# Keys and queries turned by VectorE in 32x32 pieces, pooling on VectorE, fewer GpSimd sums, maxima turned before they are loaded, a new table of places

## The chip, the cores and the metric

One core of a Trainium2 chip runs the kernel. The metric is the device time of one execution in microseconds (us); the numbers below come from three timed runs and from one more execution that was profiled.

## What is computed

Attention with queries pooled in pairs, then a mixing layer. The attention is the part that the change touches (8 batches, 8 heads, 1152 positions, 64 columns a head):

```python
q_pool = q.reshape(B, H, S // 2, 2, D).mean(axis=3)          # 576 pooled queries
scores = np.matmul(q_pool, k.transpose(0, 1, 3, 2)) / np.sqrt(D)
scores = scores - np.max(scores, axis=-1, keepdims=True)
attn = np.exp(scores)
attn = attn / (np.sum(attn, axis=-1, keepdims=True) + 1e-09)
x = np.matmul(attn, v)                                       # then laid out as 8 x 576 x 512
theta = x @ w_theta                                          # the mixing layer, untouched here
y = w_tok_r @ (x * np.cos(theta)) + w_tok_i @ (x * np.sin(theta))
u = x + y
out = u + np.maximum(u @ w_ch, 0.0)
```

## The kernel before

Two heads of one batch are a pair; there are 32 pairs, 0 to 31. A first stage does the attention of all pairs, a second the mixing layer of the 8 batches; the change lies in the first. One pair goes through these steps:

- **Loads** (SyncE, `q` L228, `k` L238, `v` L252). Pooling adds neighbouring queries: `pool_q` (L246), on VectorE for pair 0 and on GpSimd for the others.
- **Turning.** Scores need the 64 columns of a head on the partitions, so TensorE turns keys and pooled queries into PSUM (`prep_t`, tile `pt`, L277): 6 key blocks in a first group (g = 0); 6 query blocks and 3 key blocks in a second (g = 1). That is 15 matrix instructions a pair. ScalarE rounds them to `hi` (L293) and VectorE keeps the rest, `lo` (L304); two small copies make `tail` (L300).
- **Maxima** (`maxpass`, tile `pm`, L317, with VectorE's `mx`, L324, 12 blocks a pair, and `px`, `py` for the last queries). `max_nm` (L345) reduces them to 9 columns `nm` on 128 partitions, and `load_max` (L351, L352) brings these with four small DMAs into one row a head, `nmr`.
- **Scores** (`escore`, tile `pe`, L371): for each half `u` of the queries and each of 9 key tiles four products, one of which subtracts the maximum from `nmr`; ScalarE's exponential `pc` (L374). In the text a group of these 8 matmuls is a score group; there are 18 a pair.
- **Sums** (`ssum`, L383): GpSimd adds the first `TAIL` tiles of `pc` into `ss`; TensorE adds the others and sums over the keys (`norm_sum`, tile `pns`, L419).
- **Values** (`av`, tile `pa`, L397): 18 matmuls, 36 instructions, for each half. After that come the division (`xu`, L468), VectorE's 32x32 turn of the result (`xb`, L473) and the stores (L491, L494).

The order on each engine is written out by hand: each step has a place (`MAX_AT`, `PREP_AT`, `AV_AT`, `PLAN` and so on), counted in score groups from the pair's first one, 18 to a pair, and the steps are issued in the order of their places. An engine works strictly in that order. PSUM has four slots of two banks for all of it; `bank2` gives a new tile the slot that a small reckoning (`HOLD`) calls free first, so a late reader of a slot holds up whoever gets the slot next. The loads have one buffer each for `q` and `k`, two for `v`. Beside the pairs the weights of the second stage are prepared step by step (`weights`: in all 18 chunks with four VectorE operations each, L536 to L546).

Of the kernel before, what the change touches and what calls it, by code (L numbers as in the profile page):

```python
# [30 lines left out]
W_END = 30
TURN_AT = 10.275
PRO = ((-34.75, -25.8, -18.2), (-6.0, -5.0, 3.15), (3.75,))
MAX_AT0 = (-25.75, -25.25, -24.75, -24.25, -24.15, -23.25, -22.0, -21.95, -21.75, -21.25, -20.75, -20.25)
MAX_AT1 = (-22.567, -21.371, -20.761, -15.823, -13.312, -12.915, -10.876, -9.537, -8.039, -7.894, -7.714, -7.649)
PLAN = {'load_q': -54.727, 'load_k': -43.238, 'pool_q': -43.609, 'load_max': -3.244, 'load_v': -11.696, 'max_nm': -7.412, 'norm_spread': 32.09, 'norm_load': 34.755, 'norm_recip': 36.124, 'norm_save': 36.922, 'norm_bcast': 37.251, "norm_out": 46.61, "norm_turn": 46.640, 'norm_store': 56.838}
# [3 lines left out]
HOLD = {'e': (8.18, 'a', 3.247), 'pm': (4.108, 'd', 7.636), 'pt': (4.417, 'ad', 1.781), 'px': (5.029, 'd', 5.465), 'py': (6.765, 'd', 0.595), 'pa': (5.964, 'a', 0.05), 'mt': (7.562, 'a', 5.572), 'ns': (4.451, 'a', 3.778), 'pw': (2.473, 'ad', 6.596)}  # L40
# [44 lines left out]
def pooled_attention_moe_kernel(  # L85
# [114 lines left out]
    with ExitStack() as p1:  # L200
# [10 lines left out]
        nmrs = [nrm.tile([P, 5 * P], F32R, name=f"nmr_{n}") for n in range(2)]  # L211
# [12 lines left out]
        def load_q(i):  # L224
            b, hp = divmod(i, NP)
            h0 = 2 * hp
            qn = inp.tile([QP, 2, QT, 2, D], F32, tag="qn", name=f"qn{i}")
            nc.sync.dma_start(  # L228
                qn, q[b, h0 : h0 + 2].rearrange("h (p t f) d -> p h t f d", t=QT, f=2)
            )  # L230
            state[i] = dict(qn=qn)

        def load_k(i):
            b, hp = divmod(i, NP)
            h0 = 2 * hp
            kn = inp.tile([P, KT, 2, D], F32, tag="kn", name=f"kn{i}")
            for h in range(2):
                nc.sync.dma_start(kn[:, :, h, :], k[b, h0 + h].rearrange("(p t) d -> p t d", t=KT))  # L238
            state[i]["kn"] = kn

        def pool_q(i):
            qn = state[i]["qn"]
            qp = state[i]["qp"] = inp.tile([QP, QT, 2, D], F32, tag="qp", name=f"qp{i}")
            eng = nc.vector if i == 0 else nc.gpsimd
            for h in range(2):
                eng.tensor_tensor(qp[:, :, h, :], qn[:, h, :, 0, :], qn[:, h, :, 1, :], ALU.add)  # L246
# [807 lines left out]
```

## Time and profile before

| | us |
|---|---|
| median of three runs (1321.48 to 1322.57) | 1321.58 |
| the profiled execution | 1321.95 |
| its span from the first to the last instruction | 1320.2 |
| TensorE busy in the span | 1288.2 |
| VectorE busy | 847.7 |
| ScalarE busy | 665.7 |
| GpSimd busy | 895.4 |

How to read the rows further down: PE is TensorE, PEld its weight loads, DVE VectorE, ACT ScalarE, POOL GpSimd, SP SyncE. A row of windows gives, for a stretch of the span, each engine's busy time with the number of its instructions in brackets, TensorE's granted clock as a share of full speed, the mean busy share of the 16 DMA engines, and GB/s. A row of the timeline begins with the start and the duration; several instructions of one line are merged, so the distance to the next row's start tells what they cost their engine when it does not wait.

### The profile page before, as it was taken

Reading aid. Unit: us, or ns where it says so; the run is one execution under the profiler, and the core shown is the slowest. Engines: PE = TensorE matmul, PEld = TensorE weight load, DVE = VectorE, ACT = ScalarE, POOL = GpSimd, SP = SyncE. Lnnn points to the kernel's source line nnn. Section 1 sums busy time; section 2 is a strip of 40 time slices with the busy share of each in tenths; the row PEclk is TensorE's granted clock in tenths of the full one; section 3 lists DMA queues with packets and bytes.
Section 4 is the critical chain, followed back from the end, with each engine's and each line's share of the span. In section 5 each row is a group of like instructions: output and inputs, shape, how many; then the busy total and the mean of one; then the engine's idle time right before and its main releaser. Section 6 shows DMA issues by size and latency. Waiting matters only on the chain.

```text
span 1320.2 us, 29458 instructions
## 1 busy us (share of the span) xinstructions
PE 1288.2 (98%) x11850; PEld 1083.3 (82%) x11850; DVE 847.7 (64%) x1151; ACT 665.7 (50%) x1162; POOL 895.4 (68%) x664
## 2 busy tenths in 40 slices
PE   5999999999999999999999999999999999999998
PEld 3877787778787778787777777678899999999997
DVE  6766777676767686776777686545555636647452
ACT  1555555556565656565656555454443433434430
POOL 1799899999898998889998988834333333232310
PEclk7999999999999999999999999999999999999999
DMA  5335444444444444434544423225515335154231
GB/s 131 102 95 139 106 122 116 117 127 117 119 116 130 112 119 118 122 104 117 134 116 119 119 69 96 70 82 131 101 29 100 53 74 111 26 97 78 52 46 37
DMA packets 283209, 131.05 MB, mean 99 GB/s; under 512 B 247024, under 2 KB 247152, under 8 KB 283072
## 3 DMA queue, kind: packets, MB, share of 16 engines
q1 hardware_dynamic: 282896, 128.71, 40.0%
q8 instruction: 93, 1.52, 0.5%
q0 software_dynamic: 176, 0.46, 0.1%
q14 instruction: 44, 0.36, 0.1%
HBM read 97.21 MB, written 30.70 MB: 97 GB/s over the span
## 4 chain that ended last, share of the span: by engine, by line
PE 89%; DVE 4%; ACT 3%; DMA 1%; issue 1%; POOL 1%; SPq 0%; POOLq 0%; ACTq 0%; DVEq 0%
PE pe L371 21%; PE pa L397 21%; PE py L874 15%; PE pm L317 8%; PE pr L913 7%; PE pth L786 7%; PE pt L277 4%; PE pns L419 3%; DVE mx L324 2%; PE px L334 1%; ACT pc L374 1%; ACT Z L843 1%; DMA kn<-in_k_dram 0%; DMA xn<-xbd 0%; PE pwt L600 0%
## 5 line engine op out<-in xcount | busy, mean ns | idle before, releaser
L383 POOL TENSOR_TENSOR ss<-ss,pc 128x576 f32<-128x576 f32 x376 | 548.5, 1459 | 33.0 <-ACT pc L374 7.7
L324 DVE TENSOR_REDUCE mx<-pm 128x2 f32<-128x768 f32 x384 | 358.4, 956 | 204.6 <-PE pm L317 204.5
L374 ACT ACTIVATE pc<-pe 128x576 f32<-128x576 f32 x576 | 344.7, 652 | 79.1 <-PE pe L371 64.2
L397 PE MATMUL pa<-pc,vn 128*64 128x288 f32 x2304 | 294.1, 409 | 0.0
L397 PEld LDWEIGHTS pa<-pc,vn 128*64 128x64 f32 x2304 | 160.1, 137 | 119.1 <-DVE nm L345 7.4
L874 PE MATMUL py<-wtk,Z 128*128 128x288 f32 x1728 | 233.4, 295 | 0.0
L874 PEld LDWEIGHTS py<-wtk,Z 128*128 128x128 f32 x1728 | 231.9, 189 | 1.3
L847 POOL TENSOR_TENSOR Z<-ab,Z 128x512 fp32r<-128x512 f32 x40 | 52.1, 1303 | 257.3 <-ACT Z L843 242.0
L317 PE MATMUL pm<-hi 64*128 64x384 f32 x768 | 174.0, 464 | 4.7 <-ACT hi L293 2.1
L371 PE MATMUL pe<-hi 64*128 64x288 f32 x1152 | 174.1, 296 | 2.9 <-ACT pc L374 1.7
L371 PE MATMUL pe<-nmr,oner 64*128 64x288 f32 x1152 | 172.2, 292 | 1.6 <-DMA nmr<-nm 1.6
L371 PE MATMUL pe<-lo,hi 64*128 64x288 f32 x1152 | 172.2, 293 | 0.0
L371 PE MATMUL pe<-hi,lo 64*128 64x288 f32 x1152 | 172.1, 293 | 0.0
L317 PEld LDWEIGHTS pm<-hi 64*128 64x128 f32 x768 | 118.2, 306 | 35.3 <-issue 26.0
L409 ACT COPY xu<-pa 128x288 f32<-128x288 f32 x64 | 25.5, 399 | 212.9 <-PE pa L397 212.9
L371 PEld LDWEIGHTS pe<-hi 64*128 64x128 f32 x1152 | 113.6, 192 | 7.2 <-ACT pc L374 2.6
L383 POOL TENSOR_TENSOR ss<-pc,pc 128x576 f32<-128x576 f32 x64 | 92.3, 1442 | 31.9 <-ACT pc L374 31.6
L371 PEld LDWEIGHTS pe<-nmr,oner 64*128 64x128 f32 x1152 | 110.6, 185 | 2.0 <-DMA nmr<-nm 1.9
L371 PEld LDWEIGHTS pe<-hi,lo 64*128 64x128 f32 x1152 | 110.2, 185 | 0.0
L371 PEld LDWEIGHTS pe<-lo,hi 64*128 64x128 f32 x1152 | 110.0, 185 | 0.0
L913 PEld LDWEIGHTS pr<-us,wch 128*128 128x128 f32 x768 | 104.2, 189 | 1.7
L913 PE MATMUL pr<-us,wch 128*128 128x288 f32 x768 | 105.1, 295 | 0.0
(99 smaller groups left out, 1499.5 us busy)
## 6 DMA issues: line engine op xcount, KB each, us to landing
qn<-in_q_dram SPq DMA_DIRECT2D x32, 576.0 KB
kn<-in_k_dram SPq DMA_DIRECT2D x64, 288.0 KB
vn<-in_v_dram SPq DMA_DIRECT2D x32, 576.0 KB
dn<-ro SPq DMA_DIRECT2D x64, 144.0 KB
xd<-xu SPq DMA_DIRECT2D x32, 288.0 KB
xbd<-xb SPq DMA_DIRECT2D x32, 288.0 KB
xT<-xd SPq DMA_DIRECT2D x8, 1152.0 KB
xn<-xbd SPq DMA_DIRECT2D x140, 64.0 KB
```

Of the source, the lines that this page charges most:

```text
L277: nc.tensor.transpose(out=pt[:, n, c : c + R], in_=src.rearrange("p h d -> p (h d)"), identity=ident[0:R, 0:R],)
L317: nc.tensor.matmul(pm[:, h, 0:W], hi[hs, Q0 : Q0 + 4 * P].rearrange("d (p j) -> d j p", j=4)[:, j], hi[hs, K0[3 * g] : K0[3 * g] + W], sta ...
L324: nc.vector.tensor_reduce(mx[:, j : j + 5 : 4, g : g + 1], pm[:, :, 0:W], AX.X, ALU.max)
L371: nc.tensor.matmul(pe[:, h, 0:HALF], w[hs], x[hs], start=(n == 0), stop=(n == 3))
L374: nc.scalar.activation(pcs[u, kt], pe[:, :, 0:HALF], AF.Exp, scale=SC)
L383: nc.gpsimd.tensor_tensor(st["ss", u], first, st["pc"][u, kt], ALU.add)
L397: nc.tensor.matmul(pa[hs, 0, 0:HALF], st["vn"][:, h, kt, :], st["pc"][u, kt][:, h, :], start=(kt == 0), stop=(kt == KT - 1),)
L419: nc.tensor.matmul(px[a : a + 32, 1, 0:HALF], ones, sets[u][n][:, h, :], start=(n == 0), stop=(n == len(sets[0]) - 1), tile_position=(0, a),)
L786: nc.tensor.matmul(th, xs[c][:, j * P : (j + 1) * P], ws[:, c], start=(n == 0), stop=(n == 11))
L847: engine("zlo", b).tensor_tensor(Z[1], t, Z[0].bitcast(F32), ALU.subtract)
L874: nc.tensor.matmul(st["py", c, u][:, 0:HALF], Z[zi][:, c * P : (c + 1) * P], wtk[wi][:, kw, u * HALF : (u + 1) * HALF], start=(i == 0 and ...
L913: nc.tensor.matmul(pr[u][:, 0:HALF], wch[wi][:, c, e * P : (e + 1) * P], st["us", ui][:, c, u * HALF : (u + 1) * HALF], start=(n == 0), st ...
```

## The change

- Keys and queries of pairs 1 to 31 are loaded in pieces of 32 columns, so that VectorE's 32x32 turn, written straight into PSUM, gives what TensorE's 15 instructions gave: one turn of 128x768 (g = 0) and one of 128x960 (g = 1). Keys are one tile with the pooled queries, `qk`. Instead of one DMA for `q` and two for `k` there are four of each, in packets of 128 bytes. Pair 0 keeps TensorE's turn.
- The pooling of pairs 1 to 31 is one addition of 128x576 on VectorE instead of two of 96x384 on GpSimd.
- `TAIL` is 7 instead of 8: GpSimd does one addition less for each half, two a pair, and TensorE sums one set more in `pns` (not in the last pair).
- The 9 columns of maxima are turned by four 32x32 turns on VectorE (`nt`); `load_max` then reads whole rows.
- All places, the reckoning `HOLD` and the prologue have new numbers. The values' second half is split in two (4 and 5 key tiles), and `load_v` moves from 11.7 places before the pair to 9.6 behind its start.

```diff
-TAIL = 8
+TAIL = 7
-AV_AT = (((10.926, 9),), ((18.763, 9),))
+AV_AT = (((11.793, 9),), ((17.363, 4), (18.395, 5)))
...
-            qn = inp.tile([QP, 2, QT, 2, D], F32, tag="qn", name=f"qn{i}")
...
+                qn = qn[:, 0:S]
+                for h in range(2):
+                    qv = q[b, h0 + h].rearrange("(n i t) (e s) -> e i t n s", n=3, i=32, e=2)
+                    for e in range(2):
+                        a = 32 * (2 * h + e)
+                        nc.sync.dma_start(
+                            qn[a : a + 32].rearrange("i (t n s) -> i t n s", n=3, s=32), qv[e]
+                        )
...
+                kv = k[b, h0 + h].rearrange("(a i t) (e s) -> e i t a s", a=4, t=KT, e=2)
+                for e in range(2):
+                    a = 32 * (2 * h + e)
+                    nc.sync.dma_start(
+                        kn[a : a + 32].rearrange("i (t a s) -> i t a s", t=KT, a=4), kv[e]
+                    )
...
+                qv = st["qn"].rearrange("p (t f c) -> p t f c", t=QT, f=2)
+                getattr(nc, QP_ENG).tensor_tensor(
+                    qp.rearrange("p (t c) -> p t c", t=QT), qv[:, :, 0, :], qv[:, :, 1, :], ALU.add
+                )
...
+            if i > 0:
+                if g == 0:
+                    nc.vector.transpose(pt[:, :, 0 : 3 * P], kn[:, 3 * P : S])
+                else:
+                    nc.vector.transpose(pt[:, :, 0 : 5 * QP], st["q3k"])
+                return
...
-            nm = st["nm"] = sml.tile([P, KT], F32R, tag="nm", name=f"nm{i}")
-            nc.vector.tensor_reduce(nm, st["mx"], AX.X, ALU.max, negate=True)
+            nc.vector.tensor_reduce(nm[:, 0:KT], st["mx"], AX.X, ALU.max, negate=True)
+            for g in range(0, P, TB):
+                nc.vector.transpose(nt[:, g : g + TB], nm[g : g + TB])
...
-                nc.sync.dma_start(row[:, 0 : 4 * P], nm[:, 4 * h : 4 * h + 4])
-                nc.sync.dma_start(row[:, 4 * P : SQ], nm[h * HT : (h + 1) * HT, 8:9])
+                nc.sync.dma_start(row[:, 0 : 4 * P], nt[4 * h : 4 * h + 4])
+                nc.sync.dma_start(row[:, 4 * P : SQ], nt[8:9, h * HT : (h + 1) * HT])
```

On TensorE, before, this stands between the last maximum blocks of pair 13 and the first half of pair 12's values (`x6` is six instructions; the number behind a name is only a running count):

```order
L317 MATMUL pm13_32_5133<-hi13_4539 128x384 x2
L277 MATMUL pt1_14_5137<-ident_63,qp14_4755 128x96 x6
L277 MATMUL pt1_14_5137<-ident_63,kn14_4778 128x128 x3
L419 MATMUL pns11_5150<-ss0_11_4670,ones_68 32x288
...
L419 MATMUL pns11_5150<-pc11_18_4903,ones_68 32x288
L397 MATMUL pa12_0_5175<-pc12_00_4917,vn12_4668 64x288 x2
```

Now the same engine, from `px` of pair 13 on, through the second half of pair 11's values:

```order
L390 MATMUL px13_4826<-hi13_4467,tail_1_121 128x512
...
L455 MATMUL pa11_1_4834<-pc11_13_4727,vn11_4660 64x288 x2
L373 MATMUL pm13_10_4847<-hi13_4467 128x384 x2
L428 MATMUL pe12_00_4860<-hi12_4080 128x288 x2
...
L428 MATMUL pe12_00_4860<-nmr_0_116,oner_127 128x288 x2
L455 MATMUL pa11_1_4834<-pc11_14_4746,vn11_4660 64x288 x2
...
L455 MATMUL pa11_1_4834<-pc11_18_4809,vn11_4660 64x288 x2
L373 MATMUL pm13_11_4882<-hi13_4467 128x384 x2
```

The 15 turns of a pair are gone from TensorE's row, and the second half of the values, which was one block, has a maximum block and a score group of the next pair inside it.

VectorE, before, from the last maxima of pair 12 on, through a stretch with the weights' lines L169:

```order
L324 TENSOR_REDUCE mx12_4414<-pm12_32_4731 128x2
L169 TENSOR_TENSOR wtk1_79<-pwt_4735,wtk0_78 128x4x128
...
L345 TENSOR_REDUCE nm12_4770<-mx12_4414 128x9
L468 TENSOR_TENSOR xu9_4001<-xu9_4001,dn9_4597 128x576
L473 STREAM_TRANSPOSE xb9_4775<-xu9_4001 128x576
L304 TENSOR_TENSOR lo13_4540<-pt1_13_4745,hi13_4539 128x960
L324 TENSOR_REDUCE mx13_4803<-pm13_00_4804 128x2
```

Now VectorE at the same place (`pt1` and `pt0` are the turns of the second and the first group, `nt` the turned maxima):

```order
L380 TENSOR_REDUCE mx12_4364<-pm12_32_4678 128x2
L321 STREAM_TRANSPOSE pt1_13_4694<-qk13_4380 128x2x480
L400 TENSOR_REDUCE nm_124<-mx12_4364 128x9
L402 STREAM_TRANSPOSE nt_126<-nm_124 32x32 x4
L358 TENSOR_TENSOR lo13_4468<-pt1_13_4694,hi13_4467 128x960
L380 TENSOR_REDUCE mx13_4741<-pm13_00_4742 128x2
L290 TENSOR_TENSOR qk14_4757<-qn14_4476 128x576
...
L396 TENSOR_REDUCE mx13_4741<-py13_4830 128x1
L319 STREAM_TRANSPOSE pt0_14_4845<-qk14_4757 128x2x384
L380 TENSOR_REDUCE mx13_4741<-pm13_10_4847 128x2
L358 TENSOR_TENSOR lo14_4844<-pt0_14_4845,hi14_4843 128x768
```

Two large turns, four small ones and the pooling addition came into VectorE's row between the maxima; `xu` and `xb` moved behind the first group's `lo`.

SyncE, before: the values of pair 12 are asked for (L252) just ahead of pair 14's keys.

```order
L494 DMA xbd2_92<-xb8_4386 128x576
L252 DMA vn12_4668<-in_v_dram 128x2x576
L238 DMA kn14_4778<-in_k_dram 128x9x64 x2
...
L351 DMA nmr_0_116<-nm12_4770 1x128x4
```

Now SyncE at the same place:

```order
L245 DMA qn14_4476<-in_q_dram 32x36x32 x4
L540 DMA xd2_84<-xu8_3550 128x576
L543 DMA xbd2_92<-xb8_4535 128x576
L509 DMA ro9_4658<-rc9_4448 128x9
L298 DMA vn11_4660<-in_v_dram 128x2x576
L517 DMA dn9_4738<-ro9_4658 64x576 x2
L273 DMA qk14_4757<-in_k_dram 32x36x32 x4
L408 DMA nmr_0_116<-nt_126 1x4x128
```

Behind the store of pair 8's `xb` stand now the values of pair 11, where those of pair 12 stood; `q` and `k` take four issues each.

## Rows read from the trace of the kernel before

**Rows 1.** The page: busy us, share of the span and instructions of each engine.
```profile
PE 1288.2 (98%) x11850; PEld 1083.3 (82%) x11850; DVE 847.7 (64%) x1151; ACT 665.7 (50%) x1162; POOL 895.4 (68%) x664
```
**Rows 2.** Windows, all engines: the stretch of 31 pairs, and two single pairs.
```profile
69.30:864.40 795.10, 788.77 (x8373) 619.35 (x8374) 564.73 (x682) 455.60 (x816) 723.37 (x522) 1.00 0.43 114
171.90:197.60 25.70, 25.70 (x279) 20.32 (x277) 17.04 (x21) 14.10 (x26) 24.68 (x20) 1.00 0.41 106
454.10:479.70 25.60, 25.44 (x275) 20.07 (x273) 20.20 (x24) 14.88 (x27) 24.66 (x18) 1.00 0.53 138
```
**Rows 3.** Waits: engine, line, releaser: total us, times, longest.
```profile
DVE mx L324 <- PE pm L317: 204.5, 259, 3.9
```
**Rows 4.** Timeline of TensorE's matmuls over part of one pair: start, us, line.
```profile
304.21 0.71 PE L277 MATMUL pt<-ident,qp 96*128 96x96 f32 x6
...
305.18 0.69 PE L419 MATMUL pns<-ss,ones 128*32 128x288 f32 x8
305.69 0.67 PE L419 MATMUL pns<-pc,ones 128*32 128x288 f32 x8
306.29 4.59 PE L397 MATMUL pa<-pc,vn 128*64 128x288 f32 x36
310.80 0.56 PE L317 MATMUL pm<-hi 64*128 64x384 f32 x2
311.21 0.29 PE L371 MATMUL pe<-hi 64*128 64x288 f32 x2
...
311.74 0.43 PE L317 MATMUL pm<-hi 64*128 64x384 f32 x2
312.01 0.29 PE L371 MATMUL pe<-hi 64*128 64x288 f32 x2
...
316.29 0.44 PE L317 MATMUL pm<-hi 64*128 64x384 f32 x2
316.66 0.88 PE L277 MATMUL pt<-ident,kn 128*128 128x128 f32 x6
317.29 0.71 PE L334 MATMUL px<-hi,tail 128*128 128x512 f32 x3
...
317.99 4.59 PE L397 MATMUL pa<-pc,vn 128*64 128x288 f32 x36
```
**Rows 5.** Windows of line 277 alone, same 31 pairs: TensorE, PEld, clock, DMA.
```profile
69.30:864.40 795.10, 53.37 (x421) 40.85 (x420) 1.00 0.43 114
```
**Rows 6.** Windows of line 419 alone, same 31 pairs.
```profile
69.30:864.40 795.10, 38.14 (x496) 13.24 (x496) 1.00 0.43 114
```
**Rows 7.** One tile's instructions (xu): duration in ns, min/median/max.
```profile
L468 DVE TENSOR_TENSOR xu<-xu,dn x32: 740/1510/3793, 96.8 to 881.9; 128x576 f32<-128x576 f32 x32
L473 DVE STREAM_TRANSPOSE xb<-xu x32: 778/778/780, 97.7 to 882.7; 128x576 f32<-128x576 f32 x32
```
**Rows 8.** Groups by line and shape: count, busy us, mean ns, idle before.
```profile
L383 POOL TENSOR_TENSOR ss<-ss,pc 128x576 f32<-128x576 f32 x376 | 548.5, 1459 | 33.0 <-ACT pc L374 7.7
...
L304 DVE TENSOR_TENSOR lo<-pt,hi 128x960 fp32r<-128x960 f32 x32 | 36.2, 1132 | 4.6 <-ACT hi L293 4.3
...
L446 DVE RECIPROCAL rc<-rc 128x9 f32<-128x9 f32 x32 | 6.6, 205 | 5.7 <-DMA rc<-rd 5.7
```
**Rows 9.** Timeline of VectorE in the prologue: twelve maxima without a wait.
```profile
13.21 10.46 DVE L324 TENSOR_REDUCE mx<-pm 128x2 f32<-128x768 f32 x12
```
**Rows 10.** Timeline of SyncE's DMA issues: start, us, line.
```profile
305.28 1.36 SPq L238 DMA_DIRECT2D kn<-in_k_dram  x2
...
322.61 0.38 SPq L252 DMA_DIRECT2D vn<-in_v_dram  x1
```
**Rows 11.** Windows around three loads: key, four of the second stage, values' end.
```profile
306.00:310.00 4.00, 4.00 (x40) 2.23 (x34) 3.96 (x4) 1.76 (x4) 3.92 (x5) 1.00 0.75 149
1035.00:1039.00 4.00, 4.00 (x23) 3.50 (x22) 3.99 (x7) 2.59 (x4) 2.56 (x2) 1.00 0.42 66
...
326.00:327.00 1.00, 1.00 (x18) 1.00 (x16) 0.75 (x1) 0.86 (x3) 1.00 (x1) 1.00 0.01 5
```

More of the change, by code (lines that the diff above doesn't have):

```diff
@@ L31 @@
 W_END = 30
[L32 to L36, printed above, removed]
+TURN_AT = 8.506
@@ L209, in pooled_attention_moe_kernel @@
         sml = p1.enter_context(tc.tile_pool(name="sml", bufs=2))
-        nmrs = [nrm.tile([P, 5 * P], F32R, name=f"nmr_{n}") for n in range(2)]
+        nmrs = [nrm.tile([P, SQ], F32R, name=f"nmr_{n}") for n in range(2)]
         for n in range(2):
@@ L235, in load_k @@
             h0 = 2 * hp
-            kn = inp.tile([P, KT, 2, D], F32, tag="kn", name=f"kn{i}")
+            kn = keys(i)
             for h in range(2):
-                nc.sync.dma_start(kn[:, :, h, :], k[b, h0 + h].rearrange("(p t) d -> p t d", t=KT))
-            state[i]["kn"] = kn
-        def pool_q(i):
[L242 to L246, printed above, removed]
+                if i == 0:
+                    nc.sync.dma_start(
+                        kn.rearrange("p (t h d) -> p t h d", t=KT, h=2)[:, :, h, :],
+                        k[b, h0 + h].rearrange("(p t) d -> p t d", t=KT),
+                    )
+                    continue
+                kv = k[b, h0 + h].rearrange("(a i t) (e s) -> e i t a s", a=4, t=KT, e=2)
+                for e in range(2):
+                    a = 32 * (2 * h + e)
+                    nc.sync.dma_start(
+                        kn[a : a + 32].rearrange("i (t a s) -> i t a s", t=KT, a=4), kv[e]
+                    )
+        def pool_q(i):
+            st = state[i]
+            keys(i)
+            qp = st["qp"]
+            if i == 0:
+                qv = st["qn"][0:QP].rearrange("p (h t f d) -> p h t f d", h=2, t=QT, f=2)
+                ov = qp[0:QP].rearrange("p (t h d) -> p t h d", t=QT, h=2)
+                for h in range(2):
+                    nc.vector.tensor_tensor(
+                        ov[:, :, h, :], qv[:, h, :, 0, :], qv[:, h, :, 1, :], ALU.add
+                    )
+            else:
+                qv = st["qn"].rearrange("p (t f c) -> p t f c", t=QT, f=2)
+                getattr(nc, QP_ENG).tensor_tensor(
+                    qp.rearrange("p (t c) -> p t c", t=QT), qv[:, :, 0, :], qv[:, :, 1, :], ALU.add
+                )
         def load_v(i):
@@ L265, in prep_t @@
             st = state[i]
-            kn = st["kn"]
             pt = st["pt", g] = bank2("pt", f"pt{g}_{i}")
+            kn, qp = st["kn"], st["qp"]
+            if i == 0:
+                st["slot", g] = psum["slot"]
+                slots[psum["slot"]] = 1e9
+            if i > 0:
+                if g == 0:
+                    nc.vector.transpose(pt[:, :, 0 : 3 * P], kn[:, 3 * P : S])
+                else:
+                    nc.vector.transpose(pt[:, :, 0 : 5 * QP], st["q3k"])
+                return
+            kt = [kn[:, t * P : (t + 1) * P] for t in range(KT)]
             if g == 0:
-                srcs = [[kn[:, t] for t in range(3 * n, 3 * n + 3)] for n in range(2)]
+                srcs = [kt[3:6], kt[6:9]]
             else:
-                qp = st["qp"]
-                srcs = [[qp[:, t] for t in range(5)], [qp[:, 5]] + [kn[:, t] for t in (6, 7, 8)]]
+                qt = [qp[0:QP, t * P : (t + 1) * P] for t in range(QT)]
+                srcs = [qt[0:5], qt[5:6] + kt[0:3]]
             for n in range(2):
@@ L277, in prep_t @@
                     nc.tensor.transpose(
-                        out=pt[:, n, c : c + R],
-                        in_=src.rearrange("p h d -> p (h d)"),
-                        identity=ident[0:R, 0:R],
+                        out=pt[:, n, c : c + R], in_=src, identity=ident[0:R, 0:R]
                     )
@@ L304, in prep_lo @@
             nc.vector.tensor_tensor(lo, src, hi.bitcast(F32), ALU.subtract)
+            if i == 0:
+                slots[state[i]["slot", g]] = clock["d"] + 2.0
         HEADS = (slice(0, D), slice(D, P))
@@ L382, in ssum @@
             first = st["pc"][u, 0] if kt == 1 else st["ss", u]
-            nc.gpsimd.tensor_tensor(st["ss", u], first, st["pc"][u, kt], ALU.add)
+            eng = nc.vector if (u, kt) in DVE_SS else nc.gpsimd
+            eng.tensor_tensor(st["ss", u], first, st["pc"][u, kt], ALU.add)
         def av(i, u, first, n):
```

75 lines of the change are left out of this document (40 added, 35 removed).

## Prediction

> **What bounds the kernel now.** I read the page's busy times first: TensorE works for 1288.2 of 1320.2 us [rows 1]. The windows then show where. Over the 31 pairs from 69.3 to 864.4 us it is busy for 788.77 of 795.10 us at full clock, so a pair costs 795.1 / 31 = 25.65 us, and less than 0.3 us of that is idle [rows 2]. VectorE is busy for 564.73 / 31 = 18.2 us a pair, GpSimd for 23.3, ScalarE for 14.7 [rows 2]. The waits confirm it: VectorE's maxima wait 204.5 us for TensorE's blocks [rows 3]. So in the first stage time is what TensorE has to do. An instruction taken from it shortens the pair, as long as VectorE, which gets the work, still answers in time; it has 7.4 us a pair to spare. The mixing layer behind it isn't touched.
>
> **What leaves TensorE.** The timeline gives the turns' price as distances between starts [rows 4]: the second group from 304.21 to 305.18 is 0.97 us, the first from 316.66 to 317.29 is 0.63, together 1.60 a pair. Counted as busy time it would be 53.37 us for 421 instructions, at 15 a pair 1.90 [rows 5], but that holds the tails under which the next work starts; 1.60 is my value, 1.90 the upper end. Going into a turn costs too: the maximum block ahead of it takes from 316.29 to 316.66, 0.37 instead of the usual 0.27 (311.74 to 312.01) [rows 4], twice 0.10 a pair. 31 pairs lose these: 31 x 1.80 = 55.8 us.
>
> **What comes to TensorE.** One more set of sums for 31 pairs. The first set takes 0.51 us (305.18 to 305.69), the second with the change to the values 0.60 [rows 4]; as busy time 38.14 / 31 / 2 = 0.62 [rows 6]. I take 0.53: 16.4 us. The second half of the values is cut in two. Behind such a block a maximum block takes 0.41 (310.80 to 311.21) instead of 0.27 [rows 4], and going in should cost about what going into a turn costs, 0.10: 0.24 a pair, 7.4 us. Net on TensorE: 55.8 - 16.4 - 7.4 = 32.0 us less, and a pair of 24.6 us. With the upper prices it is 31 x (1.90 + 0.20 - 0.53 - 0.14) = 44, with the lower (0.62 a set, nothing saved going in) 31 x (1.60 - 0.62 - 0.24) = 23.
>
> **What comes to VectorE.** No row shows a turn into PSUM. From SBUF to SBUF 576 columns take 778 ns [rows 7], the 9 columns of the reciprocal 205 [rows 8]; that is 1.01 ns a column, so 0.97 us for 768 and 1.16 for 960. Operations that follow each other without a wait overlap a little: twelve maxima take 10.46 us [rows 9], 0.87 each, which I allow for with 2.0 us for the two. If writing to PSUM halved the pace, 1728 more columns would cost 1.7 us more, 3.7. Nothing could make them cheaper than the count of columns, 1.75. The four small turns: between 0.2 and 0.8 us by the 205 ns row; I take 0.6, near the upper end, as they are four instructions. The pooling addition has the shape of `xu`, 128x576 from two tiles in SBUF: 0.74 at best, 1.51 at the median, 3.79 at worst [rows 7]. The spread has one visible reason, GpSimd, which is busy 91% of the time [rows 2]. That engine loses two sums of 1.46 us [rows 8] and the pooling, so it will be busy about three quarters of the time; I take 1.1 us. VectorE gets 3.7 us a pair: 18.2 + 3.7 = 21.9 of 24.6 us, 89%. Not all pairs are alike: without weights' work it is 17.0, with it 20.2 [rows 2], so 20.7 and 23.9. The second is close.
>
> The Trainium skill (SBUF — State Buffer, Who interferes with whom) says that a VectorE instruction with two SBUF inputs and a GpSimd instruction that reads SBUF exclude each other for a whole instruction; the spread from 740 to 3793 ns agrees. By it the pooling addition can wait for a whole sum each time; that is the first rival.
>
> **Does VectorE answer in time?** I laid one pair out by hand, with time 0 where the first half of the values starts. TensorE: values to 4.5 us, a score group (0.53 each, 311.21 to 311.74), maximum block `pm00` to 5.3, three groups, `pm01` to 7.2, two groups, `pm02` to 8.5, then `px` to 9.2 (0.70, 317.29 to 317.99), eight matmuls of values to 11.2, `pm10` [rows 4]. VectorE, from the last maximum of the pair before: `mx32` done at 0.7, the turn of 960 at 1.8, `nm` and its turns at 2.5, `lo` behind ScalarE's rounding at 4.1 (1.13 us, [rows 8]), `mx00` at 6.4, the pooling at 7.5, `mx01` at 8.4, `mx02` at 9.6, `px` near 11, the turn of 768 near 12. The slots rotate: `px` needs the slot that `mx01` frees, 8.4 against 8.5; `pm10` the one that `px` frees. It just fits, with nothing lost. With weights' work (3.2 us more, most of it ahead of `mx02`) `mx01` comes at about 8.9, and TensorE waits 0.4 us; later blocks have slack again, as VectorE catches up behind `mx12`. There are 18 chunks of weights, so 18 x 0.4 = 7 us.
>
> **Loads.** The keys' 2304 packets of 256 bytes keep the DMA engines busy for 0.75 x 4 us x 16 = 48 us in sum [rows 11], 20.8 ns a packet. Four loads of the second stage (64 KB each, 2048 packets of 128 bytes) keep them busy for 0.42 x 4 x 16 = 27 us [rows 11], 13.1 ns a packet. The keys are now 4608 of these, 3.8 us on 16 engines instead of 3.0. Four issues of 0.68 us (1.36 for two, [rows 10]) run beside it. They start when the turn of 960 ends, at 1.8, and before, from issue to the last byte took 310 - 305.3 = 4.7 us [rows 10, 11]: landed at about 8, and the turn of 768 wants them at 11. The query load has nearly a pair. Maxima: the load is issued behind the keys, 5 to 7.5, and the first score group of the next pair wants it at 12. All this stays covered; without the cover each late us costs a us in 31 pairs. The values: below. In the prologue VectorE turns pair 1 ahead of the maxima's load of pair 0, 2 us later, and TensorE is spared 15 turns there; I count it as nothing, 3 us either way.
>
> **Sum.** The profiled execution took 1321.95 us, 0.4 above the median. 1321.95 - 32.0 + 7 = **1297 us**, 1.9% faster.
>
> **Rivals.**
> 1. VectorE becomes the bound in the pairs with weights. The pooling addition waits 1.0 us longer, or the turns take nearer to 3.7 than 2.0. Then every one of the 18 chunks costs 1.0 us more and the other 13 pairs some 0.2: 1297 + 18 + 3 = **1318**. For it: 23.9 of 24.6 us. Against it: GpSimd gets 5 us a pair less to do, and `xu` may gain from that what the pooling loses.
> 2. The values come late; this one ends slower. SyncE issues `load_v` now behind the stores of `xu` and `xb`, and so behind VectorE's `xb`, near 16.7 in the pair by my layout, for a use at 24.6. Before, it had more than a pair. The issue follows at about 17.4; before, the bytes were in at 326.0 for an issue at 322.61 [rows 10, 11], 3.4 us. That is 21, with 3 us to spare. If DMAs of stores and weights ahead of it, or a late VectorE, eat these 3 us, TensorE waits with all that stands behind the values. Each us costs 31; from 25 / 31 = 0.8 us late the change is slower than before. At 1 us late: 1297 + 31 = **1328**.
> 3. The keys come late, or ScalarE's rounding behind VectorE's turn does, and VectorE stands with the maxima behind it. That takes 3 us more than reckoned; at 4.5 us it costs 1.5 x 31 = 47: **1344**. The packet's price speaks against it.
> 4. VectorE never holds TensorE up, and the turns cost their busy time [rows 5]: 31 x (1.90 + 0.20 - 0.53 - 0.24) = 41, so **1281**. For it: the present order keeps TensorE's idle time below 0.3 us a pair.
>
> **Chances.** The forecast (1286 to 1309) 0.63, rival 1 0.14, rival 2 0.08, rival 3 0.05, rival 4 0.10. The range of 8 in 10 takes the forecast, most of rival 1 and the near part of rival 4: 1283 to 1321. About 0.2% is what a measurement of this kernel can tell from no change, 2.6 us. Faster: 0.63 + 0.10 and half of rival 1, 0.80; within 0.2%: 0.05; slower: rivals 2 and 3 and a bad case of rival 1, 0.15.
>
> **What would show it.** Right: TensorE's line of turns shrinks to one pair's, `pns` has 24 records a pair, a pair takes 24.5 to 25.2 us and TensorE stays above 97% busy; VectorE near 22 us a pair, its turns near 0.97 and 1.16 us; GpSimd near 18. Rival 1 shows as score groups or maximum blocks that wait for `mx`, in pairs with weights; rival 2 as `pa` waiting for the DMA of `vn`; rival 3 as a VectorE turn waiting for the DMA of `qk`. I am wrong if TensorE's idle time grows by more than 0.8 us a pair, or if turning it off saves less than 1.5 us there.

## The result, and the profile after

The changed kernel took **1291.88 us** (median of four runs, 1289.72 to 1293.1) against 1321.8 us of the kernel before (also four runs) on the same chip: a ratio of 0.977, with a 95% interval of 0.9754 to 0.9788. The forecast was 1297, the range 1283 to 1321. The time lies in the range. Two terms were wrong, however, one on each side (one isn't in the sum at all), and they nearly cancel, which is luck; most of the experiments are about these two.

The profiled execution took 1291.21 us, with a span of 1289.4. Busy times first, from the page; they answer to [rows 1]:

```profile
PE 1239.3 (96%) x11633; PEld 1006.3 (78%) x11633; DVE 943.7 (73%) x1373; ACT 673.2 (52%) x1162; POOL 749.3 (58%) x540
```

VectorE has 96 us more and GpSimd 146 less, as intended. TensorE has 49 us less. The windows over 31 pairs, from the first `pns` to the last one, show it pair by pair, before (first row) and after (second row). Behind the length of the stretch stand the busy time and the count of TensorE, its weight loads, VectorE, ScalarE and GpSimd, then the granted clock, the share of the DMA engines and GB/s:

```profile
69.30:866.40 797.10, 790.77 (x8387) 620.33 (x8386) 565.39 (x682) 455.60 (x816) 723.37 (x522) 1.00 0.43 114
```

```profile
67.40:836.30 768.90, 751.02 (x8239) 552.60 (x8237) 654.94 (x890) 465.04 (x819) 588.69 (x409) 1.00 0.55 119
```

A pair went from 797.1 / 31 = 25.71 us to 768.9 / 31 = 24.80, so 31 x 0.91 = 28.2 us of the gain lie here; another 1.9 lie ahead of the first `pns` (69.3 against 67.4) and 0.7 behind the last. The clock is full in both. VectorE has 654.94 / 31 = 21.1 us a pair, GpSimd 19.0.

What the page says of the maximum blocks was not in my sum. Two rows of before, then the two of after; the last columns are busy us, mean ns of one instruction, and idle time ahead of them:

```profile
L317 PE MATMUL pm<-hi 64*128 64x384 f32 x768 | 174.0, 464 | 4.7 <-ACT hi L293 2.1
L317 PEld LDWEIGHTS pm<-hi 64*128 64x128 f32 x768 | 118.2, 306 | 35.3 <-issue 26.0
```

```profile
L373 PE MATMUL pm<-hi 64*128 64x384 f32 x768 | 146.4, 379 | 16.0 <-ACT hi L347 5.8
L373 PEld LDWEIGHTS pm<-hi 64*128 64x128 f32 x768 | 73.6, 188 | 64.0 <-DVE mx L380 16.2
```

The same matmul of the same shape, but its weight load takes 188 instead of 306 ns. The weights are 128 queries. Before, a block took every fourth query (16 bytes apart in `hi`), because `load_max` needed the maxima in that order; now that VectorE turns the maxima, it takes 128 neighbours. In the timeline of after, the distance from such a block to the next group is 0.17 us (305.02 to 305.19), where it was 0.27 in [rows 4]:

```profile
305.02 0.34 PE L373 MATMUL pm<-hi 64*128 64x384 f32 x2
305.19 0.30 PE L428 MATMUL pe<-hi 64*128 64x288 f32 x2
```

Twelve blocks a pair: 12 x 0.10 x 31 = 37 us that I did not count. Without any other error the time would have been 1321.95 - 32.0 - 37 = 1253 us. So some 39 us are lost elsewhere, where I had allowed 7. To see where, I add up the distances between TensorE's starts over the 31 pairs of both traces, each distance put to the tile that begins it. The turns' 45.7 us are gone; the sums take 11.0 us more (38.7, then 49.7) and the values 4.7 more (281.2, then 285.9). The maximum blocks take only 20.6 us less (111.2, then 90.6), and the score groups, which are the same groups, 20.4 us more (294.3, then 314.7; some 6 of these are the cut of the values, which is in my sum). So the loss lies behind the maximum blocks and in the score groups. A part of it shows as idle time of TensorE, which grew from 797.10 - 790.77 = 6.3 us to 768.90 - 751.02 = 17.9. The list of what TensorE waited for names some of it (us in total, times, longest):

```profile
PE px L390 <- DVE mx L380: 9.7, 18, 0.6
...
PE pa L455 <- DMA vn<-in_v_dram: 5.2, 4, 1.9
...
PE pm L373 <- DVE mx L380: 3.6, 9, 0.8
```

And VectorE's maxima, which waited 204.5 us for TensorE's blocks [rows 3], now wait 81.0:

```profile
L380 DVE TENSOR_REDUCE mx<-pm 128x2 f32<-128x768 f32 x384 | 356.9, 953 | 82.9 <-PE pm L373 81.0
```

That is the sign to read: the engine that used to wait has become nearly as late as the one it waited for. It depends on the pair. These are two of after, one with the weights' operations on VectorE and one without; VectorE's busy time is the third in each row, 23.55 of 25.15 us and 20.24 of 24.94. TensorE is idle for 0.74 us in the first and not at all in the second:

```profile
169.02:194.17 25.15, 24.41 (x270) 17.90 (x269) 23.55 (x33) 15.79 (x29) 17.27 (x13) 1.00 0.59 124
194.17:219.11 24.94, 24.94 (x275) 18.41 (x274) 20.24 (x29) 14.97 (x26) 20.57 (x15) 1.00 0.56 117
```

### The profile page after: what moved, and what is told of

It reads as the page before. It is cut to its first block, busy times and chain, and to the rows that moved or that the text cites. A ratio compares the mean times of both kernels' runs of the same rounds, so it can differ in the third digit from the quotient of the medians.

```text
span 1289.4 us, 29397 instructions
## 1 busy us (share of the span) xinstructions
PE 1239.3 (96%) x11633; PEld 1006.3 (78%) x11633; DVE 943.7 (73%) x1373; ACT 673.2 (52%) x1162; POOL 749.3 (58%) x540
## 4 chain that ended last, share of the span: by engine, by line
PE 78%; DVE 10%; DMA 5%; ACT 2%; issue 2%; POOL 1%; SPq 1%; DVEq 0%; POOLq 0%; ACTq 0%
PE pa L455 20%; PE pe L428 18%; PE py L917 16%; PE pr L956 8%; PE pth L829 7%; PE pm L373 5%; DVE mx L380 4%; PE pns L477 3%; DMA vn<-in_v_dram 2%; DMA nmr<-nt 1%; DVE qk L290 1%; PE px L390 1%; DVE wf L591 1%; DVE mx L395 1%; DMA qk<-in_k_dram 1%
## 5 line engine op out<-in xcount | busy, mean ns | idle before, releaser
L441 POOL TENSOR_TENSOR ss<-ss,pc 128x576 f32<-128x576 f32 x314 | 463.8, 1477 | 53.9 <-ACT pc L431 33.6
L431 ACT ACTIVATE pc<-pe 128x576 f32<-128x576 f32 x576 | 349.8, 652 | 74.0 <-PE pe L428 64.0
L455 PE MATMUL pa<-pc,vn 128*64 128x288 f32 x2304 | 300.4, 410 | 5.5 <-DMA vn<-in_v_dram 5.2
L428 PE MATMUL pe<-hi 64*128 64x288 f32 x1152 | 181.8, 311 | 0.3 <-DVE lo L358 0.2
L373 PE MATMUL pm<-hi 64*128 64x384 f32 x768 | 146.4, 379 | 16.0 <-ACT hi L347 5.8
L428 PEld LDWEIGHTS pe<-hi 64*128 64x128 f32 x1152 | 109.1, 185 | 23.8 <-issue 8.8
L373 PEld LDWEIGHTS pm<-hi 64*128 64x128 f32 x768 | 73.6, 188 | 64.0 <-DVE mx L380 16.2
L347 ACT CAST hi<-pt 128x768 fp32r<-128x768 f32 x64 | 56.3, 880 | 114.5 <-DVE pt L319 105.7
```

The source lines that it names most:

```text
L347: nc.scalar.copy(hi, src)
L373: nc.tensor.matmul(pm[:, h, 0:W], hi[hs, Q0 + j * P : Q0 + (j + 1) * P], hi[hs, K0[3 * g] : K0[3 * g] + W], start=True, stop=True,)
L428: nc.tensor.matmul(pe[:, h, 0:HALF], w[hs], x[hs], start=(n == 0), stop=(n == 3))
L431: nc.scalar.activation(pcs[u, kt], pe[:, :, 0:HALF], AF.Exp, scale=SC)
L441: eng.tensor_tensor(st["ss", u], first, st["pc"][u, kt], ALU.add)
L455: nc.tensor.matmul(pa[hs, 0, 0:HALF], st["vn"][:, h, (kt + 3) % KT, :], st["pc"][u, kt][:, h, :], start=(kt == 0), stop=(kt == KT - 1),)
```

## The experiments

All were run beside the kernel before; each time is a median of at least four runs, and the ratios in brackets are to the kernel before on the same chip. Two changed kernels are compared by their medians, partly from different chips, on which the kernel before took between 1321.3 and 1322.1 us. "After" is the changed kernel (1291.9), "before" the old one (1321.8).

### The weights with and without a stride: `a_strided`, `b_max`

After, with the old order of queries as weights (each query then subtracts another query's maximum; the work is the same):

```diff
-                            hi[hs, Q0 + j * P : Q0 + (j + 1) * P],
+                            hi[hs, Q0 : Q0 + 4 * P].rearrange("d (p j) -> d j p", j=4)[:, j],
```

> The changed kernel, but the maximum blocks take every fourth query as their weights again, as the kernel before did (the order of the maxima in their row is left as in the changed kernel, so the subtracted maxima belong to other queries, which the division cancels). Theory: weights read with a stride cost TensorE 0.10 us a block, 12 blocks a pair, 37 us in 31 pairs; as TensorE now waits part of the time for VectorE, some of it is swallowed: 1301 to 1329 us, about 1310. Rival (the longer weight load is hidden beneath the matmuls and the narrower distance between blocks comes from elsewhere): 1292 us, no change against the changed kernel.

Measured: 1311.53 us (0.9918, 0.9903 to 0.9934). The weight loads are back at the old time:

```profile
L373 PE MATMUL pm<-hi 64*128 64x384 f32 x768 | 183.0, 476 | 13.9 <-ACT hi L347 5.8
L373 PEld LDWEIGHTS pm<-hi 64*128 64x128 f32 x768 | 118.7, 306 | 60.3 <-DVE mx L380 14.5
```

The stride alone costs 19.6 us, so it decides two thirds of the whole gain; about half of the 37 us doesn't arrive. With the longer blocks TensorE is idle for 10.4 us of the 31 pairs instead of 17.9:

```profile
68.50:857.77 789.27, 778.87 (x8239) 590.66 (x8237) 654.17 (x890) 465.79 (x819) 587.50 (x409) 1.00 0.54 116
```

The opposite experiment puts only the part with the maxima into the kernel before: neighbouring queries, the turn of `nm` on VectorE and whole rows in `load_max`.

```diff
-                            hi[hs, Q0 : Q0 + 4 * P].rearrange("d (p j) -> d j p", j=4)[:, j],
+                            hi[hs, Q0 + j * P : Q0 + (j + 1) * P],
...
+            nc.vector.tensor_reduce(nm[:, 0:KT], st["mx"], AX.X, ALU.max, negate=True)
+            for g in range(0, P, TB):
+                nc.vector.transpose(nt[:, g : g + TB], nm[g : g + TB])
...
```

> The kernel before with the maxima's part of the change alone: 128 neighbouring queries as weights, the nine columns turned by VectorE in four 32x32 turns, whole rows loaded. Nothing else is changed, the places neither. Theory: TensorE is the bound there and loses 12 x 0.10 us a pair, 32 pairs: 1322 - 38 = 1284 us, less than the whole change takes; VectorE has 18.2 + 0.8 of 24.5 us. Rival (the stride costs nothing that counts): 1320 to 1322 us.

Measured: 1301.45 us (0.9844, 0.9827 to 0.9862), 20.6 us less and not 38. So the direction holds and the size doesn't. The two halves add up, by their ratios: the change without the neighbouring queries brings 0.8%, the part with the maxima alone 1.6%, together 2.4%, and the whole change 2.3%.

### What swallows the rest: `c_dve`, `c_act`, `a_dve`

In `b_max` the 17 missing us are only in part visible as idle time, which grew by 4.6 us. Others lie inside instructions. TensorE's timeline, at a score group like all others and at one that is held:

```profile
305.81 0.30 PE L376 MATMUL pe<-hi 64*128 64x288 f32 x2
305.94 0.30 PE L376 MATMUL pe<-lo,hi 64*128 64x288 f32 x2
...
306.33 0.39 PE L376 MATMUL pe<-hi 64*128 64x288 f32 x2
306.56 0.29 PE L376 MATMUL pe<-lo,hi 64*128 64x288 f32 x2
```

The distance from the first to the second row is 0.13 us in the usual group and 0.23 in the other. VectorE at that time (two maxima in one row, 0.96 for the first):

```profile
305.31 1.82 DVE L328 TENSOR_REDUCE mx<-pm 128x2 f32<-128x768 f32 x2 [0.38 <-PE pm L321]
```

The first maximum ends at 305.31 + 0.96 = 306.27, 0.06 us ahead of the held group, which is the fourth tile behind that maximum's block (304.82) and so takes the slot that it frees. Counting in the trace every first matmul of a group whose next row comes more than 0.17 us later gives 12 of them over the 31 pairs in before, 127 in `b_max` (12.3 us over the usual distance) and 94 in after (10.0 us).

Not all of these are held by VectorE. The trace tells which semaphore each waited for last. In `b_max` it is a maximum's in 106 of them, a `lo`'s in 9 and an exponential's in 8. In after it is different. There 33 of the 94 stand directly behind a block of values, as every such group does, also the three in before: its first distance is always 0.24 us, so that is the price of leaving the values and no hold. Of the other 61 a maximum releases 29 and one of ScalarE's exponentials 30. In `a_strided`, with the longer blocks, the 33 are there and only 2 others: the holds of after come with its shorter blocks.

Two kernels ask which engine frees the slot late, by making one engine's answers shorter, at the price of a part of the computation, and leaving TensorE's work as it is. `c_dve` is `b_max` with

```diff
-                        mx[:, j : j + 5 : 4, g : g + 1], pm[:, :, 0:W], AX.X, ALU.max
+                        mx[:, j : j + 5 : 4, g : g + 1], pm[:, :, 0:256], AX.X, ALU.max
```

> The maxima part alone (b_max) brought 20.6 us where the shorter weight loads are worth about 38 on TensorE. In its trace the first matmul of a score group starts on time but lasts 388 instead of 291 ns in 127 groups of the first stage (12 in the kernel before); those I looked at start 0.06 us after one of VectorE's maxima ends, so they wait for the PSUM slot that this maximum frees. This kernel is b_max with VectorE's maxima over 256 of the 384 columns of each block (a part of the computation left out: a maximum takes about 0.65 instead of 0.96 us); TensorE's, ScalarE's and GpSimd's instructions are the same. Theory (VectorE's answer holds the slot): most of the 127 holds go and the time falls by 8 to 14 us, to 1287 to 1294. Rival (ScalarE's pace of 0.63 us a group in the runs of groups without values): the holds stay, 1299 to 1303.

and `c_act` is `b_max` with

```diff
+PART = 144
...
-            nc.scalar.activation(pcs[u, kt], pe[:, :, 0:HALF], AF.Exp, scale=SC)
+            nc.scalar.activation(pcs[u, kt][:, :, 0:PART], pe[:, :, 0:PART], AF.Exp, scale=SC)
...
```

and the sums and the values read the 144 columns twice (those lines are left out here).

> b_max with ScalarE's exponential over 144 of the 288 columns of each half (a part of the computation left out: about 0.37 instead of 0.63 us a group); the values, the sums and GpSimd read the 144 columns twice, so that their instructions keep their sizes. Theory (VectorE's answer holds the slot): the holds stay, 1298 to 1303. Rival (ScalarE's pace): the holds go, and the time falls by 8 to 14 us, to 1287 to 1294. If both help by half, each slot is taken in turn by both engines and no single one can be named.

| | us | a maximum, ns | an exponential, ns | held groups |
|---|---|---|---|---|
| `b_max` | 1301.45 | 955 | 652 | 127 |
| `c_dve` | 1284.16 (1282.36 to 1287.41) | 691 | 652 | 22 |
| `c_act` | 1294.24 (1294.16 to 1294.57) | 956 | 412 | 123 |

Shorter maxima bring 17.3 us, more than the theory's 8 to 14, and the held groups go (10.0 of the 17.3 us). In the profiled executions 13.8 us of it lie in the 31 pairs (778.7, then 764.9); another 3.7 lie ahead of the first `pns`, where maxima stand in a row, and have nothing to do with the holds. Shorter exponentials bring 7.2 us, a little under what the rival asked for and more than the theory allowed, and the held groups stay, so these are VectorE's. ScalarE has a part in the rest that I can't place, and since the two edits were not measured together, how much of the 17.3 is VectorE's alone stays open. Shorter maxima in the kernel before, where hardly a group is held, were not run; they would tell what such maxima bring without any holds.

The same edit on the changed kernel:

> The changed kernel with VectorE's maxima over 256 of the 384 columns of each block (a part of the computation left out: about 0.69 instead of 0.95 us a maximum, 3.1 us a pair less on VectorE); TensorE's, ScalarE's and GpSimd's instructions are the same. Reckoned on TensorE alone the change would be worth 32 us by my sum and some 37 by the shorter weight loads, which would give 1253; measured 1292. Theory (what is missing waits for VectorE's answers, above all for its maxima): the time falls by 20 us or more, to 1250 to 1272, and the first matmuls of score groups that last 388 ns fall from 94 to under 30. Rival (it waits for something else: values, ScalarE's rounding, the loads): 1280 or more.

Measured: 1271.84 us (0.9619, 0.9603 to 0.9635), 20.0 us less. The time is at the near end of what the theory asked for; the held groups fell from 94 only to 65, not under 30. What went are the 29 that a maximum releases; the 33 behind values and ScalarE's 30 are still there. In the profiled executions 14.8 us of the gain lie in the 31 pairs (768.9, then 754.1) and 3.1 ahead of the first `pns`. The same two pairs as above, with shorter maxima:

```profile
163.28:187.44 24.16, 24.16 (x269) 17.86 (x268) 19.69 (x33) 15.70 (x29) 17.49 (x13) 1.00 0.62 130
187.44:212.30 24.86, 24.86 (x275) 18.38 (x273) 17.60 (x29) 15.07 (x26) 20.38 (x15) 1.00 0.59 119
```

The pair with weights is 0.99 us shorter, the other 0.08. Over all, the 14 pairs with more than 2.4 us of weights' operations on VectorE gain 0.69 us each, the other 17 on the mean 0.30. So shorter answers of VectorE bring back 14.8 of the 39 us, most of it in pairs with weights. The values' load is another 3.7 (below). Some 20 us of the 39 stay without a name; ScalarE's 30 holds are about 3 of them.

### VectorE's load and the values' place: `a_poolg`, `a_vearly`, `a_pg_vearly`

```diff
-QP_ENG = 'vector'
+QP_ENG = 'gpsimd'
```

> The changed kernel with the pooling addition of 128x576 on GpSimd instead of VectorE. Theory: VectorE, 21.1 us busy of 24.8 in a pair, holds TensorE up, and 1.3 us less there gives back up to that: 1260 to 1285 us, about 1278. Rival (TensorE's own work or the loads set the pair): 1290 to 1294 us, or more, as GpSimd gets 1.5 us a pair in front of its sums.

Measured: 1284.18 us (0.9715, 0.9699 to 0.973), 7.7 less than after. The pooling addition, 747 to 1795 ns on VectorE, costs the pair more there than on GpSimd, which has time now: the waits of `px` for `mx`, 18 in after (9.7 us, shown above), are one of 0.3 us here. For the values:

```diff
-PLAN = {..., 'load_v': 9.606, ...}
+PLAN = {..., 'load_v': 0.0, ...}
```

> The changed kernel with the load of the values asked for 9.6 places earlier, ahead of the two result stores on SyncE instead of behind them. Theory: the profile of the changed kernel has the load of the values in its chain with 2% and four direct waits of together 5.2 us; these go and little else: 1283 to 1288 us. Rival (the wait only takes the place of one for VectorE that would come anyway): 1291 to 1293 us.

Measured: 1288.23 us (0.9751, 0.9737 to 0.9764), 3.7 less. That is near the noise: the interval overlaps with after's (0.9754 to 0.9788). In after the load stands in SyncE's queue behind the store of `xb`:

```profile
316.75 0.33 SPq L543 DMA_DIRECT2D xbd<-xb  x1
...
318.30 0.39 SPq L298 DMA_DIRECT2D vn<-in_v_dram  x1
```

TensorE waits for these values only now and then (four waits, 5.2 us, shown above); early, it doesn't wait at all. Both edits together:

> The changed kernel with both: pooling on GpSimd and the values asked for ahead of the stores. Theory: the two gains add, 7.7 and some 5: 1276 to 1281 us. Rival (both removed the same wait): 1284 us, as with the pooling alone.

Measured: 1280.55 us (0.9692, 0.9678 to 0.9705). The gains add up to 11.3 us, and with the pooling on GpSimd the earlier load brings 3.6 again. This is the fastest of all that compute the whole, and better than both kernels.

### The price of the turn: `a_peturn`, `a_pe_poolg`

`a_peturn` lets TensorE turn for all pairs, as before, with the loads in rows that this needs and the pooling in two additions on VectorE, and keeps all places:

```diff
+PETURN = True
...
-            if i > 0:
+            if not PETURN and i > 0:
```

> The changed kernel with TensorE's turn for all pairs, keys and queries loaded in rows as in the kernel before, pooling still on VectorE (two of 96x384); all places as in the changed kernel. Theory: the turns cost TensorE 1.6 to 1.8 us a pair, but VectorE loses 2.1 us and no longer holds TensorE up (1.6 us a pair are lost to waits in the changed kernel): a pair of 25.0 to 25.2 us instead of 24.8, about 1300 us. Rival (the waits have nothing to do with VectorE's load): the full price, 1292 + 31 x 1.7 = 1345 us.

Measured: 1396.83 us (1.0571, 1.0549 to 1.0593): far worse than both theories. The waits say where:

```profile
PE px L391 <- DVE mx L381: 49.2, 27, 2.2
```

With keys and queries loaded in rows the pooling is two additions of 96x384, and in VectorE's order they stand ahead of the second maximum, here for 3.28 us:

```profile
458.68 3.28 DVE L286 TENSOR_TENSOR qk<-qn 96x384 f32<-96x384 f32 x2
```

A kernel that moves only these two to GpSimd tells this from "the new places don't suit TensorE's turn":

```diff
-                    nc.vector.tensor_tensor(
+                    (nc.vector if i == 0 else nc.gpsimd).tensor_tensor(
```

> The changed kernel with TensorE's turn for all pairs and pooling on GpSimd as before (two of 96x384), to be compared with the changed kernel with pooling on GpSimd (1284 us); all places as in the changed kernel. Theory: the turns' full price on TensorE, 31 x 1.7 = 53 us, less a little that VectorE's 2.1 us give back: 1325 to 1337 us. Rival (what made the earlier run with TensorE's turn slow, 1397 us, was not the pooling's wait on VectorE but the places themselves): 1370 us or more.

Measured: 1328.06 us (1.0044, 1.003 to 1.0058). So 69 us of `a_peturn` were the pooling on VectorE. The 49.2 us of waits are gone (0.3 are left), and the mean granted clock over the profiled span is 0.998, where it was 0.982 in `a_peturn`. Against `a_poolg`, which differs by the turn, its loads and the shape of GpSimd's pooling (one addition of 128x576 there), it is 43.9 us slower: 1.42 us a pair for 31 pairs. That is what moving the turns is worth in this order.

### One more set on TensorE, and the cut of the values: `a_tail8`, `a_pgv_whole`

```diff
-TAIL = 7
+TAIL = 8
```

> The changed kernel with 8 tiles summed on GpSimd instead of 7, as before. Theory: TensorE is spared 0.5 us a pair (16 us in all), of which VectorE's and the loads' waits give back the larger part, and GpSimd, 2.9 us a pair fuller, holds up VectorE's additions from two SBUF tiles more often: 1283 to 1295 us. Rival A (TensorE's own work alone sets the pair): 1276 us. Rival B (GpSimd's sums come late for TensorE's): 1300 us or more.

Measured: 1295.6 us (0.9805, 0.9792 to 0.9818), 3.7 slower than after, although TensorE has less to do (its sums take 39.2 us of the 31 pairs instead of 49.7): that is swallowed and more. The theory, up to 1295 us, had the larger part swallowed, so it falls just short. With two more sums a pair GpSimd is again busy for 88% of the first stage (682.5 of 780 us), and VectorE's `xu`, at the same places as in after, has a median of 1428 ns, where it has 749 in after:

```profile
L526 DVE TENSOR_TENSOR xu<-xu,dn x32: 734/1428/1894, 111.7 to 855.6; 128x576 f32<-128x576 f32 x32
```

TensorE's waits for the values rise from 5.2 to 8.9 us; which other waits take the rest I did not follow.

`a_pgv_whole` is `a_pg_vearly` with the second half of the values in one piece:

```diff
-AV_AT = (((11.793, 9),), ((17.363, 4), (18.395, 5)))
+AV_AT = (((11.793, 9),), ((17.363, 9),))
```

> The changed kernel with pooling on GpSimd and the values' load early (1280.6), and the second half of the values whole instead of cut in two. My price for the cut was 0.24 us a pair on TensorE, 7.4 us. If that holds and nothing stands behind it: 1272 to 1275. If the maximum block that stood in the cut was what gave VectorE and ScalarE time to answer, waits swallow it: 1278 to 1286.

Measured: 1349.15 us (1.0212, 1.0197 to 1.0227), 68.6 slower than `a_pg_vearly`; neither theory had anything like it. ScalarE's timeline, then VectorE's, behind the block of values:

```profile
303.71 0.40 ACT L467 COPY xu<-pa 128x288 f32<-128x288 f32 x1 [4.68 <-PE pa L455]
304.00 0.81 ACT L347 CAST hi<-pt 128x768 fp32r<-128x768 f32 x1
```

```profile
304.64 0.96 DVE L380 TENSOR_REDUCE mx<-pm 128x2 f32<-128x768 f32 x1 [3.24 <-PE pm L373]
305.52 0.94 DVE L358 TENSOR_TENSOR lo<-pt,hi 128x768 fp32r<-128x768 f32 x1
```

With one block of values ScalarE's copy of the result (`xu`) comes ahead of the rounding `hi` in ScalarE's row; in the cut version, `a_pg_vearly`, `hi` comes ahead of it:

```profile
305.80 0.80 ACT L347 CAST hi<-pt 128x768 fp32r<-128x768 f32 x1 [2.94 <-DVE pt L319]
...
308.59 0.40 ACT L467 COPY xu<-pa 128x288 f32<-128x288 f32 x1 [1.44 <-PE pa L455]
```

So, with one block, `hi`, and with it VectorE's `lo`, waits until the values are through, and TensorE's next score group waits for `lo`:

```profile
306.52 0.61 PE L428 MATMUL pe<-hi 64*128 64x288 f32 x2 [1.22 <-DVE lo L358]
306.92 0.44 PE L428 MATMUL pe<-lo,hi 64*128 64x288 f32 x2
```

```profile
PE pe L428 <- DVE lo L358: 41.3, 30, 1.9
PE pm L373 <- ACT xu L467: 14.5, 29, 0.5
```

30 waits, 41.3 us; the maximum block behind the values waits for the copy itself, 14.5 us more. With the clock's 19 (last section), less what undoing the cut spares TensorE, that is about what was lost. So the cut is not only a price for one more way into and out of the values; by this trace it keeps a chain of three engines off the path. A kernel that moves the copy alone was not run, and the cut also enters the reckoning of the slots, so the chain is read from the trace and not proved.

## Why the prediction came out right, and where it was wrong

- **TensorE loses its turns (55.8 us reckoned): right, a little large.** Its row has only pair 0's left. By the distances it held 45.7 us, and 0.09 more at each of 47 maximum blocks ahead of it, together about 50. The turn was worth 43.9 us in `a_pe_poolg` against `a_poolg`, after what VectorE's turns hold up; that is 1.42 us a pair, under the 1.5 that I had named as the point where I would be wrong on this term.
- **One more set of sums (16.4): right.** The windows of L477 alone show 745 records over 31 pairs, 24 a pair, and the timeline takes 0.51 us for the first eight (320.00 to 320.51). `a_tail8` shows that the exchange with GpSimd was worth making.
- **The split of the values (7.4): about right.** Undoing it made the kernel 68.6 us slower by another mechanism, which hides what the cut costs TensorE. But the timeline of after shows its two parts: a score group ahead of values takes 0.64 us instead of 0.53, and the one behind them 0.10 more; 31 x 0.21 = 6.5 us.
- **The weights of the maximum blocks: missed.** I read the part with the maxima as four small turns on VectorE and another load, and didn't see that the order of the queries in the blocks changes with it. It is worth 37 us on TensorE's own time, 19.6 in the end. The row was in front of me as [rows 4]: two matmuls of 384 columns cost 0.27 us, 0.35 ns a column, where a score group of eight of 288 costs 0.53, 0.23 ns a column. After, the block costs 0.17, 0.22 ns a column.
- **VectorE's instructions: right.** Here are the two large turns, the pooling addition, the small turns and `xu` (min, median and max in ns, first and last start):

```profile
L319 DVE STREAM_TRANSPOSE pt<-qk x31: 973/983/984, 25.5 to 763.5; 128x768 f32<-128x768 f32 x31
```

```profile
L321 DVE STREAM_TRANSPOSE pt<-qk x31: 1148/1183/1194, 26.4 to 777.0; 128x960 f32<-128x960 f32 x31
```

```profile
L290 DVE TENSOR_TENSOR qk<-qn x31: 747/1472/1795, 14.8 to 757.7; 128x576 f32<-128x576 f32 x31
```

```profile
L402 DVE STREAM_TRANSPOSE nt<-nm x128: 199/199/204, 27.6 to 802.7; 32x32 f32<-32x32 f32 x128
```

```profile
L526 DVE TENSOR_TENSOR xu<-xu,dn x32: 737/749/1869, 110.4 to 851.8; 128x576 f32<-128x576 f32 x32
```

  The turns into PSUM take 0.98 and 1.18 us (0.97 and 1.16 reckoned), so writing there costs next to nothing extra. The pooling lies nearer to the median of [rows 7] than the 1.1 us that I took. In exchange the median of `xu`, the same shape, fell from 1510 [rows 7] to 749 ns, with GpSimd busy for 77% instead of 91% of the stretch. This goes with GpSimd's load and not with the new place, for in `a_tail8`, at the same places and with GpSimd at 88%, it is 1428 again. For this the rule of the Trainium skill that I had cited (SBUF — State Buffer, Who interferes with whom) points the same way. In sum 21.1 us a pair instead of 21.9.
- **VectorE's answers (7 us reckoned): the step that failed.** I asked whether VectorE has time and whether each block finds a slot, laid out one pair with 12 blocks at the old distances, and found 0.4 us in pairs with weights. The busy times of that layout were right (20.2 and 23.6 us in the two pairs above, 20.7 and 23.9 reckoned); the old distances were not. With blocks that come 0.10 us earlier each, the slots run out more often. Against `a_strided`, which has the longer blocks, TensorE's idle time is 17.9 us instead of 10.4, and 61 groups are held instead of 2, a half of them by VectorE and a half by ScalarE, which my layout left out. Shorter maxima bring back 14.8 us in the 31 pairs. TensorE is still busy for 751.0 of 768.9 us, 97.7%, and that was one of my signs of being right; it says little, since a held matmul counts as busy.
- **Rival 1 (VectorE becomes the bound): half true.** Its mechanism is there, and mostly in the pairs that it named: 0.69 us come back by shorter maxima in those with most weights. But the other pairs lose 0.30 too, and the 7.7 us that came back with the pooling on GpSimd are not tied to the weights (0.25 us in a pair without any, 0.14 in the 14 with most). **Rival 2 (values late): true in small**, 3.7 us instead of 31. **Rival 3 (keys late)** did not come in the first stage: no turn of VectorE shows a wait for the DMA of `qk`, though packets of under 512 bytes rose from 247024 to 451744. **Rival 4** took for granted that VectorE never holds TensorE up, which its waits and 29 of the held groups deny.
- **The prologue (0, plus or minus 3):** 1.9 us gained.

So the time was close by luck: the missed 37 us stand against some 32 us of waits and holds that I didn't foresee. Had I seen the stride alone, I would have said 1260 and been further off.

## What to carry to other kernels

When an operand's order changes, price the instructions that read it again, weight loads too: a stride is not in the shape. When TensorE is the bound and its blocks get shorter, ask next how long the answers of the engines that free its PSUM slots take, and look for the loss inside the matmul rows (the distance between starts), not only in the idle time. And an instruction that is moved or cut also changes the order on the engines that answer it; in `a_pgv_whole`, 69 us slower, 55.8 us of TensorE's waits lie behind one copy that came ahead of one rounding.

## What was not expected of the hardware

- A weight load of 64x128 values that lie 16 bytes apart takes 306 ns, and of neighbouring ones 188, in both kernels with the stride (before and `a_strided`) and in after and `b_max` without; the matmul behind it shows 464 and 476 ns against 379 in after.
- A first matmul of a score group that finds its slot just freed shows 388 instead of 291 ns; the distances show 0.10 us each, over a hundred times alike in `b_max`. A group directly behind a block of values has the same look without any hold, in all 33 cases of after.
- In `a_pgv_whole` TensorE's clock fell after the waits. The windows of that kernel, with the granted clock in the third column from the end:

```profile
304.00:306.40 2.40, 1.14 (x12) 0.86 (x12) 1.76 (x3) 1.46 (x3) 1.28 (x1) 1.00 0.98 153
306.40:309.40 3.00, 2.88 (x24) 2.88 (x26) 2.38 (x5) 1.15 (x2) 0.72 (x1) 0.52 0.95 221
309.40:313.00 3.60, 3.60 (x52) 3.50 (x50) 2.25 (x3) 2.97 (x6) 3.44 (x3) 0.93 1.04 390
```

  TensorE was busy for 1.14 of 2.40 us in the first window; in the next the clock is 0.52, near the lower of its two levels (1.2 of 2.4 GHz), and a score group takes 0.96 us (307.64 to 308.60) instead of 0.53. So this wait of 1.2 us cost, as an estimate, about another 1.3 behind it (three groups of 0.43 more). Over the whole span the mean granted clock is 0.984, against 0.998 in `a_pg_vearly`: 0.014 x 1347 = 19 us by estimate, beside the 41.3 us of waits for `lo`.
